# Taking weight remainders off GpSimd and laying out the order anew: attention, dense block and routed experts in one kernel

## The chip, the cores and the metric

The kernel runs on one core of a Trainium2 chip. The core has five engines with queues of their own: TensorE (PE in the profile, with PEld for its weight loads), VectorE (DVE), ScalarE (ACT), GpSimd (POOL) and SyncE (SP), which issues most of the transfers. The metric is the time of one execution on the device in microseconds, the median of several runs.

## The reference, cut to what matters

Three stages follow one another. Linear attention runs a state over 768 positions for 4 batches and 8 heads of 48. Its output, 3072 tokens of 384, goes through a dense block with a softplus between two matrices (384x2048 and 2048x384, given in double precision). Then every token is given to one of 8 experts with room for 384 tokens each, in the order of falling scores, and the expert's two matrices (384x1024 and 1024x384, with a relu) make the output.

```python
for t in range(S):                        # attention
    cur = np.einsum('bhd,bhe->bhde', u[None] * kt, vt)
    y[:, :, t] = np.einsum('bhd,bhde->bhe', rt, state + cur)
    state = w[None, :, :, None] * state + np.einsum('bhd,bhe->bhde', kt, vt)
...
h = x @ w_in                              # dense block
g = np.maximum(h, 0.0) + np.log1p(np.exp(-np.abs(h)))
x = g @ w_out
...
for idx in np.argsort(-logits.flatten()): # routing
    tok, e = (int(idx) // E, int(idx) % E)
    if assigned[tok] >= 0 or counts[e] >= cap:
        continue
    assigned[tok] = e
    counts[e] += 1
...
h = np.maximum(x[mask] @ w1[e], 0.0)      # one expert
out[mask] = h @ w2[e]
```

## The kernel before, in words

**Attention.** The 768 positions are cut into chunks of 64. One step handles a chunk for two batches, so there are 24 steps; step n belongs to token block n // 3 of the dense block (three steps, 384 tokens). A step loads r, k and v (`load_step`, on SyncE's queue), scales them with powers of the decay, turns them on TensorE, and forms the products of keys and queries inside the chunk: `prods`, line 524, 32 small matmuls. `masked` multiplies these products with a triangular mask on VectorE. For steps below `WHOLE` the products of both batches land in one half of the partitions and each of the two heads of a pair is masked by one instruction of 64x512 (line 532); for the later steps they are spread over both halves and masked by two instructions of 64x256 (line 537). Line 607 then makes the step's output, and lines 558 and 565 carry the state on.

**Dense block.** `ffn1` (lines 743 and 748) and `ffn2` (lines 855 and 858 to 860) run over 8 blocks of 384 tokens. Block 0 uses the weights in 32 bits, the later blocks use halves: a 16-bit value and a 16-bit remainder, three matmuls for one. The raw double-precision weights are loaded by SyncE and turned into 32 bits by three bit operations each on VectorE (lines 655, 657 and 659). The last twelve pieces of `ffn2` are kept for later (`LATE`): they fill TensorE while the routing starts.

**Routing and experts.** `select` runs eight rounds, one for each expert that is closed. A round is a chain of short VectorE instructions and small matmuls (lines 1108 and 1125) that finds the score at which the expert is full; then the chosen tokens are numbered and the numbering is inverted into a token list (VectorE lines 1205, 1196 and 1199, matmuls of line 1214, list at line 1223). The last round needs no search. `gather` fetches the listed rows with GpSimd (line 1277), SyncE transposes them (line 1352), `up` (line 1364) and `down` (lines 1382 to 1384) are the expert's matmuls, and `scatter` (line 1392) writes the rows out with GpSimd. `weights` loads an expert's matrices in eight tiles. ScalarE makes the 16-bit value of a tile (`hi`, line 1311), and VectorE the remainder (`lo`, line 1318). In rounds 6 and 7, for the seven tiles that `ON_POOL` names, it is otherwise: ScalarE scales the tile in place (line 1308) and casts it (line 1309), and GpSimd subtracts (line 1316).

**Order.** Every step is an `Item` with an engine (or a choice of ScalarE and VectorE), a planned duration, dependencies and a due time. `lay_out` is a list scheduler: it takes the engine that can start first and, of its items that can start within `SLACK`, the one that is due first. An item with a choice is delayed on an engine by `YIELD` and by `BIAS` times what the engine is slower. While a GpSimd item runs the plan doesn't start VectorE items on SBUF, unless the item is marked `remote`. The due times are made of the constants that stand in the code: `T0`, `LEN0`, `LEN` and `LAST` for the dense blocks, `STEP` and `SPAN` for the selection rounds and experts, and leads that end in L (`RAWL` for the raw loads of the dense weights, `BITL` for their bit operations, `HIL`, `LOL` and `FETCHL` for the experts' weights, `INVL` for the inversion). The order that comes out is written into the queues of the engines; on the chip each engine keeps it. Where the plan sees a gap on TensorE, `keep_warm` puts filler matmuls of 128x128 into it (line 143).

Of the kernel before, what the change touches and what calls it, by code (L numbers as in the profile page):

```python
# [14 lines left out]
OP = mybir.AluOpType  # L15
# [6 lines left out]
def tile_kernel(ctx, tc, r, k, v, w, u, w_in, w_out, w_gate, w1, w2, out):  # L22
# [18 lines left out]
    PE, ACT, DVE, POOL, SP = nc.tensor, nc.scalar, nc.vector, nc.gpsimd, nc.sync  # L41
# [11 lines left out]


    LAT = 150.0
    SLACK = 82.556
    SAME = {"dve": 130.0, "act": 150.0}
    NBANK = 7
    BIAS = 1.348
    YIELD0 = 247.951  # L60
    YIELD = {"dve": YIELD0}
    WARM = 1e9
    LPH = 6
# [45 lines left out]
    def op(eng, dur, fn, r=(), w=(), due=0.0, lat=None, bank=None, size=0.0, small=False):  # L109
        deps = []  # L110
        if lat is None:
            lat = LATA[0] if GROUP[0] == "att" else LAT
        for key in r:
            deps.append(writer.get(key))
        for key in w:
            deps.append(writer.get(key))
            deps += readers.get(key, [])
        for b in banks_of(bank):
            deps += b.items
        it = Item(eng, dur, fn, deps, due, lat, [b for b in banks_of(bank) if not b.items], bank, size)  # L120
        for b in banks_of(bank):
            if eng == "pe":
                b.items = [it]
            b.items = b.items[:1] if eng != "pe" else b.items
            b.all.append(it)
        it.small = small
        for key in r:
            readers.setdefault(key, []).append(it)
        for key in w:
            writer[key] = it  # L130
            readers[key] = []
        return it
# [115 lines left out]
        return 2 * pair, c * C  # L248


    T0 = 22576.265
    LEN0 = 52137.908
    LEN = 27173.331
    NLATE = 12
    EARLY = 0.549
    LATE = [divmod(NB * SPB - NLATE + i, SPB) for i in range(NLATE)]
    LAST = 21924.657


    SLOT = [0, 1, 2, 0, 1, 2, 0, 3]  # L260
# [1 line left out]
    def begins(blk):  # L262
        return T0 if blk <= 0 else T0 + LEN0 + (blk - 1) * LEN

# [6 lines left out]
            return ATT0 * t  # L271
        return begins(blk - 1) + lasts(blk - 1) * t / SPB - (AHEAD if blk > 1 else 0.0)

    AHEAD = 14956.929

    TURNED, TURN = 6, 1500.0
    WHOLE = 9
    SINGLE = 2
    COPIED = 6
    HALFL = 4425.245  # L280
    HALFL2 = 4963.628
    NLAT = 6
    LATL = 155.16
    OUTLATE = 12980.585
    RAWL = 12886.281
    BITL = 9483.311
    SPLITL = -3900.0
    WOUTL = 8511.548
    ATT0 = 2213.113
    LOADL = 1908.468  # L290

    base = begins(NB - 1) + LAST + 1000.0

# [47 lines left out]
    gate = work.tile([128, KC, 32], FT, name="gate")  # L341
# [24 lines left out]
    def load_step(n):  # L366
# [25 lines left out]
    wt = const.tile([128, HP], FT, name="wt")  # L392
    ut = const.tile([128, H * D], FT, name="ut")
    jp = keep.tile([128, 128], I32, name="jp")
    identf = keep.tile([128, 128], FT, name="identf")
    identh = keep.tile([128, 128], HF, name="identh")
    mask = const.tile([128, C], FT, name="mask")
# [10 lines left out]
                              for q in range(2)], w=["uq"], due=-1000.0, size=168.0)  # L408
    op("sp", 450.0, lambda: SP.dma_start(
        ut, bass.AP(tensor=u.tensor, offset=u.offset, ap=[[0, 128], [1, H * D]])), w=["ut"], due=due_att(3), size=1200.0)  # L410
    op("pool", 200.0, lambda: POOL.memset(gate, 0.0), w=["gate"], due=-1e9)
    op("sp", 450.0, lambda: SP.dma_start(gate[:, :, :E], w_gate.rearrange("(k p) e -> p k e", p=128)),
       w=["gate"], due=T0, size=168.0)
    op("pool", 100.0, lambda: POOL.iota(jp, pattern=[[1, 128]], base=0, channel_multiplier=-1), w=["jp"], due=-1e9)
# [1 line left out]
        for t in RS + KS:  # L416
            POOL.memset(t[:, :, D:], 0.0)

    op("pool", 700.0, pads, w=["pads"], due=-1e9)

    def masks():
        POOL.tensor_scalar(mask[0:64], jp[0:64, 0:64], 0.0, None, op0=OP.is_gt)
        POOL.tensor_scalar(mask[64:128], jp[64:128, 64:128], 0.0, None, op0=OP.is_gt)
        POOL.tensor_copy(identh, identf)

    op("pool", 800.0, lambda: POOL.tensor_scalar(identf, jp, 0.0, None, op0=OP.is_equal), r=["jp"], w=["ident"], due=-1e9)
    op("pool", 1500.0, masks, r=["jp", "ident"], w=["mask"], due=-1e9)


    def powers():  # L430
# [21 lines left out]
            DVE.tensor_mul(uw[q * 64:q * 64 + D, :, q], uq[q * 64:q * 64 + D], wt[q * 64:q * 64 + D])  # L452

    op("dve", 300.0, factors, r=["wt", "uq"], w=["uw"], due=2.5)
    op("dve", 1700.0, powers, r=["wt"], w=["pw", ("ar", 1, 0)], due=-1e8)

    def power_table(i):
        bank = Bank("att")
# [16 lines left out]
    def attention(n):  # L475
# [10 lines left out]
        if n % PC == 0:  # L486
            def zero():
                POOL.memset(X[x][0:64, 0], 0.0)
                POOL.memset(X[x][64:128, 1], 0.0)
            op("pool", 700.0, zero, w=[("st", x, 0), ("st", x, 1)], due=due)  # L490


        b1, b2 = Bank("att"), Bank("att")
# [34 lines left out]
        def masked(q):  # L528
            o = 1 - q
            if n < WHOLE:  # L530
                rows = slice(o * 64, (o + 1) * 64)
                DVE.tensor_mul(ar[rows, :, :, q, :], b3[q].view(HP, 2, 64)[rows],
                               mask[rows, None, None, :].to_broadcast([64, HP, 2, 64]))
                return
            for b in range(2):
                rows = slice(b * 64, (b + 1) * 64)
                DVE.tensor_mul(ar[o * 64:(o + 1) * 64, :, b, q, :], b3[q].view(HP, 64)[rows],
                               mask[rows, None, :].to_broadcast([64, HP, 64]))

        op("pe", 825.0 if n < WHOLE else 625.0, prods, r=[("kT", i), ("ar", i, 0), ("ar", i, 1)], w=[("am", i, 0), ("am", i, 1)], due=due + 3, bank=b3, small=True)  # L540
        for q in range(2):
            op("dve", 600.0 if n < WHOLE else 890.0, lambda q=q: masked(q), r=["mask"], w=[("am", i, q)], due=due + 3, bank=b3[q])


        if n % PC < PC - 1:
# [286 lines left out]

    NG = 1
    none = flat[0:64, 28:30].rearrange("p f t -> p (f t)")
    op("pool", 800.0, lambda: POOL.memset(none, 0.0), w=["none"], due=begins(0))
    for i in range(2 * NG):
        b0, s0 = step_tok(NS - NG + i // 2)
        X2S.append(op("sp", 650.0, lambda row=(b0 + i % 2) * S + s0: SP.dma_start(x2d[row:row + 64, :], none),
# [159 lines left out]
    def item(eng, dur, fn, deps, prio, lat=LAT, size=0.0, bank=None):  # L998
        take = [b for b in banks_of(bank) if not b.all]
        it = Item(eng, dur, fn, deps, prio, lat, take, bank, size)  # L1000
        for b in banks_of(bank):
            b.all.append(it)
        return it
# [4 lines left out]

    WQ, WB, RB = 4, 6, 4
    FIRST = 10500.0 + 8000.0 * NLATE  # L1010
    STEP = 21647.984
    SPAN = 23783.33

    ON_POOL = [()] * 6 + [(0, 1, 2, 3, 4, 5, 7)] * 2
    XLEAD = -13221.524
    GLEAD = 11385.847
    FETCHL = 13257.035
    W1L = -2788.168
    W2L = -1812.505
    HIL = 11584.279  # L1020
    LOL = 8711.69
    DOWNL = 7740.516
    INVL = -8223.999
    PUT = []
    IDX, EST, TK = {}, {}, {}
    SEL, WI, GI = {}, {}, {}
# [257 lines left out]
    def weights(p):  # L1284
        W[p] = [[None, None] for _ in range(2 * WQ)]
        z = {}

        def load():
            z["e"] = SP.value_load(EST[p][0:1, 0:1], min_val=0, max_val=E - 1)

        def fetch(y):
            e = z["e"]
            if y < WQ:
                q = F2 // WQ
                src = w1[bass.ds(e, 1)].rearrange("o (k p) f -> p (o k) f", p=128)[:, :, y * q:(y + 1) * q]
                sh = [128, KC, q]
            else:
                q = FB // WQ
                src = w2[bass.ds(e, 1)].rearrange("o (c p) m -> p (o c) m", p=128)[:, (y - WQ) * q:(y - WQ + 1) * q]
                sh = [128, q, DM]  # L1300
            z["raw", y] = moe.tile(sh, FT, name="mraw", bufs=RB)
            SP.dma_start(z["raw", y], src)
            z["sh", y] = sh

        def hi(y):
            W[p][y][0] = moe.tile(z["sh", y], HF, name="w1h" if y < WQ else "w2h", bufs=WB)
            if y in ON_POOL[p]:
                ACT.mul(z["raw", y], z["raw", y], 128.0)
                ACT.copy(W[p][y][0], z["raw", y])
            else:  # L1310
                ACT.mul(W[p][y][0], z["raw", y], 128.0)

        def lo(y):
            W[p][y][1] = moe.tile(z["sh", y], HF, name="w1l" if y < WQ else "w2l", bufs=WB)
            if y in ON_POOL[p]:
                POOL.tensor_tensor(W[p][y][1], z["raw", y], W[p][y][0], op=OP.subtract)
            else:
                DVE.scalar_tensor_tensor(W[p][y][1], z["raw", y], 128.0, W[p][y][0], op0=OP.mult, op1=OP.subtract)

        ld = item("sp", 700, load, [SEL[p][1], more_room], begin(p) - 15000)  # L1320
        WI[p] = []
        for y in range(2 * WQ):
            k = len(raws)
            old = raws[k - RB] if k >= RB else None
            want = begin(p) + (2930 * y - W1L if y < WQ else W2L + 2930 * (y - WQ))
            f = item("sp", 450, lambda y=y: fetch(y), [ld, old], want - FETCHL, size=1700)
            g = p * WQ + y % WQ - WB
            if g >= 0:
                gp, gz = divmod(g, WQ)
                wold = W1R[gp, gz] if y < WQ else W2R[gp, gz]  # L1330
            else:
                wold = []
            h = item("act", 1680 if y in ON_POOL[p] else 740, lambda y=y: hi(y), [f] + wold, want - HIL)
            if y in ON_POOL[p]:
                l = item("pool", 1660, lambda y=y: lo(y), [h] + wold, want - LOL)
            else:
                l = item("dve", 880, lambda y=y: lo(y), [h] + wold, want - LOL)
            raws.append(l)
            WI[p].append(l)

# [150 lines left out]
```

## Time and profile before

| | us |
|---|---|
| median of 3 runs | 761.86 |
| lowest and highest | 761.34, 764.19 |
| the profiled execution | 759.91 |
| its span, first to last instruction | 758.1 |
| TensorE busy in it | 741.5 |
| VectorE busy | 595.1 |
| ScalarE busy | 424.2 |
| GpSimd busy | 85.2 |

The profile is of one execution. Busy times of TensorE are of pipelined matmuls, so a matmul of 384 columns is shown with about 0.33 us though one starts every 0.16 us; a TensorE that is busy throughout is not for that reason at its peak. In the views below the time at the start of a row is counted from the span's start, the time behind it is the duration, and a bracket at the end names idle time of the engine just before and what ended it.

### The profile page before, as it was taken

The numbers are of one execution on the slowest core, as the hardware profiler recorded it, in microseconds if no ns is written. First come the engines' busy times: TensorE is split into PE (matmuls) and PEld (weight loads), VectorE is DVE, ScalarE is ACT, GpSimd is POOL, SyncE is SP. The second block draws the span as 40 slices with busy tenths as digits, with TensorE's granted clock in tenths as the row PEclk, the third lists the DMA queues.
The fourth block names the chain that finished last, engine by engine and source line by source line (L and its number), as shares of the span: only waits on it lengthen the run. The fifth ranks groups of instructions, "written<-read, shape, count | busy, mean of one in ns | idle before, by whom it ended". The sixth has DMA issues, their size and how long they took to land.

```text
span 758.1 us, 18115 instructions
## 1 busy us (share of the span) xinstructions
PE 741.5 (98%) x7144; PEld 489.2 (65%) x7144; DVE 595.1 (79%) x1594; ACT 424.2 (56%) x859; POOL 85.2 (11%) x114
## 2 busy tenths in 40 slices
PE   9999999999999999999999999999999999997996
PEld 8767766666666666667666666666666666664663
DVE  6899999998777777778988768787798889984220
ACT  4586766776766666668989702120343533462741
POOL 2000000000000000000001000000532122145641
PEclk9999999999999999999999999999999999998998
DMA  5896884243333333331110005142487382855810
GB/s 107 194 214 164 163 204 114 48 84 74 64 64 63 64 64 64 63 64 34 32 23 2 1 22 151 59 146 74 102 196 204 107 231 92 219 159 134 208 53 32
DMA packets 164853, 78.86 MB, mean 104 GB/s; under 512 B 130464, under 2 KB 160416, under 8 KB 164768
## 3 DMA queue, kind: packets, MB, share of 16 engines
q1 hardware_dynamic: 161696, 68.26, 38.9%
q0 software_dynamic: 3072, 9.44, 3.9%
q8 instruction: 56, 0.92, 0.5%
q14 instruction: 29, 0.24, 0.1%
HBM read 60.37 MB, written 9.63 MB: 92 GB/s over the span
## 4 chain that ended last, share of the span: by engine, by line
PE 71%; DVE 15%; issue 5%; DMA 3%; POOL 2%; ACT 2%; SPq 1%; POOLq 0%; DVEq 0%; ACTq 0%
PE bank L748 19%; PE bank L1364 9%; PE bank L858 6%; PE bank L860 6%; PE bank L859 6%; PE bank L1382 3%; PE bank L1383 3%; PE bank L1384 3%; PE bank L607 2%; PE bank L1108 2%; PE bank L855 2%; PE bank L524 1%; DMA third<-moe_w_in 1%; PE bank L558 1%; SPq L373 1%
## 5 line engine op out<-in xcount | busy, mean ns | idle before, releaser
L748 PEld LDWEIGHTS <-wi 128*128 128x128 f16 x1008 | 97.9, 98 | 66.0 <-issue 2.3
L748 PE MATMUL bank<-xt,wi 128*128 128x384 f16 x672 | 127.6, 326 | 0.1
L754 ACT ACTIVATE ta<-bank 128x384 f32<-128x384 f32 x128 | 61.4, 483 | 36.3 <-PE bank L748 25.1
L761 DVE SCALAR_TENSOR_TENSOR gf<-bank,ta 128x384 f32<-128x384 f32 x112 | 61.4, 550 | 21.9 <-ACT ta L756 21.6
L858 PE MATMUL bank<-wo,g 128*128 128x384 f16 (+1 forms) x240 | 78.5, 327 | 0.0
L860 PE MATMUL bank<-wo,g 128*128 128x384 f16 (+1 forms) x240 | 78.5, 327 | 0.0
L859 PE MATMUL bank<-wo,g 128*128 128x384 f16 (+1 forms) x240 | 78.4, 327 | 0.0
L748 PE MATMUL bank<-xs,wi 128*128 128x384 f16 x336 | 72.9, 326 | 0.0
L1364 PE MATMUL bank<-g,w1h 128*128 128x384 f16 x384 | 72.9, 326 | 0.0
L755 ACT ACTIVATE ta<-ta 128x384 f32<-128x384 f32 x128 | 66.4, 522 | 2.5
L756 ACT ACTIVATE ta<-ta 128x384 f32<-128x384 f32 x128 | 66.2, 521 | 2.2
L1382 PE MATMUL bank<-w2h,g 128*128 128x384 f16 x192 | 63.7, 332 | 0.0
L1383 PE MATMUL bank<-w2l,g 128*128 128x384 f16 x192 | 63.7, 332 | 0.0
L1384 PE MATMUL bank<-w2h,g 128*128 128x384 f16 x192 | 63.6, 331 | 0.0
L1368 ACT ACTIVATE g<-bank 128x384 f16<-128x384 f32 x64 | 31.2, 489 | 41.2 <-PE bank L1364 24.7
L768 DVE SCALAR_TENSOR_TENSOR g<-gf,g 128x384 f16<-128x384 f32 x80 | 43.9, 552 | 11.3 <-ACT g L351 10.8
L1364 PEld LDWEIGHTS <-w1h 128*128 128x128 f16 x384 | 35.7, 98 | 22.1
L351 ACT ACTIVATE x2o<-bank 128x384 f16<-128x384 f32 x24 | 11.6, 489 | 67.5 <-PE bank L860 41.5
L1371 DVE SCALAR_TENSOR_TENSOR g<-bank,g 128x384 f16<-128x384 f32 x64 | 34.0, 548 | 18.9 <-ACT g L1368 18.8
L1277 POOL DMA_INDIRECT third<-x2d,idx x24 | 27.6, 1151 | 156.7 <-PE bank L1125 132.3
L351 ACT ACTIVATE g<-gf 128x384 f16<-128x384 f32 x66 | 34.3, 520 | 16.2 <-DVE gf L761 16.0
L1364 PE MATMUL bank<-g,w1l 128*128 128x384 f16 x192 | 41.7, 326 | 0.0
(237 smaller groups left out, 1511.6 us busy)
## 6 DMA issues: line engine op xcount, KB each, us to landing
mraw<-moe_w SPq DMA_DIRECT2D x64, 384.0 KB, 3.9
third<-moe_w_in SPq DMA_DIRECT2D x16, 384.0 KB, 4.7
third<-moe_w_out SPq DMA_DIRECT2D x8, 768.0 KB, 4.8
kn<-k SPq DMA_DIRECT2D x48, 96.0 KB, 3.0
rn<-r SPq DMA_DIRECT2D x48, 96.0 KB, 3.4
vn<-v SPq DMA_DIRECT2D x48, 96.0 KB, 3.0
x2d<-x2o SPq DMA_DIRECT2D x48, 96.0 KB, 2.2
X<-v SPq DMA_DIRECT2D x36, 96.0 KB, 3.4
```

Source lines behind the costliest of these rows:

```text
L748: PE.matmul(ph, WF[:, f, a, kk, :], x[:, kk, :], start=(i == 0), stop=(i == 3 * KC - 1))
L754: op("act", 371.0, lambda: ACT.activation(ta, bank.view(BT), AF.Abs), w=[("ta", c)], due=due, bank=bank)
L755: op("act", 413.0, lambda: ACT.activation(ta, ta, AF.Exp, scale=-1.0), w=[("ta", c)], due=due)
L756: op("act", 413.0, lambda: ACT.activation(ta, ta, AF.Ln, bias=1.0), w=[("ta", c)], due=due)
L761: op("dve", 470.0, lambda: DVE.scalar_tensor_tensor(gf, bank.view(BT), 0.0, ta, op0=OP.max, op1=OP.add), r=[("ta", c)], w=[("gf", c)], due ...
L858: PE.matmul(p, gh[:, f, ts], WU[:, f, 0, :no], start=(f == 0), stop=False)
L859: PE.matmul(p, gh[:, f, ts], WU[:, f, 1, :no], start=False, stop=False)
L860: PE.matmul(p, gl[:, f, ts], WU[:, f, 0, :no], start=False, stop=(f == FC - 1))
L1364: PE.matmul(ph, a[:, kk, fs], XH[p][:, x0 + kk, :], start=(i == 0), stop=(i == 3 * KC - 1))
L1382: PE.matmul(po, h1h[:, f, js], w2h[:, fz, :], start=(f == 0), stop=False)
L1383: PE.matmul(po, h1h[:, f, js], w2l[:, fz, :], start=False, stop=False)
L1384: PE.matmul(po, h1l[:, f, js], w2h[:, fz, :], start=False, stop=(f == FB - 1))
```

## The change

The change takes the remainders of rounds 6 and 7 from GpSimd: `ON_POOL` is gone, and all tiles are made as in rounds 0 to 5, one ScalarE instruction and one VectorE instruction. `WHOLE` goes from 9 to 3, so that steps 3 to 8 use the products and masks of the later steps. The planned durations of seven kinds of item are new, four memset items are marked `remote`, and 29 constants of the ordering have new values. The computation is otherwise the same, instruction by instruction, but for what the planner chooses anew: order, engine of the items with a choice, and filler.

```diff
-    SLACK = 82.556
+    SLACK = 106.939
-    BIAS = 1.348
-    YIELD0 = 247.951
+    BIAS = 2.396
+    YIELD0 = 49.069
...
-    T0 = 22576.265
-    LEN0 = 52137.908
-    LEN = 27173.331
+    T0 = 22458.956
+    LEN0 = 56876.682
+    LEN = 30310.245
...
-    WHOLE = 9
+    WHOLE = 3
...
-    RAWL = 12886.281
-    BITL = 9483.311
+    RAWL = 17811.751
+    BITL = 3671.703
...
-    LOADL = 1908.468
+    LOADL = -407.377
...
-    op("pool", 200.0, lambda: POOL.memset(gate, 0.0), w=["gate"], due=-1e9)
+    op("pool", 200.0, lambda: POOL.memset(gate, 0.0), w=["gate"], due=-1e9).remote = True
...
-    op("pool", 700.0, pads, w=["pads"], due=-1e9)
+    op("pool", 700.0, pads, w=["pads"], due=-1e9).remote = True
...
-    op("pool", 800.0, lambda: POOL.tensor_scalar(identf, jp, 0.0, None, op0=OP.is_equal), r=["jp"], w=["ident"], due=-1e9)
-    op("pool", 1500.0, masks, r=["jp", "ident"], w=["mask"], due=-1e9)
+    op("pool", 560.0, lambda: POOL.tensor_scalar(identf, jp, 0.0, None, op0=OP.is_equal), r=["jp"], w=["ident"], due=-1e9)
+    op("pool", 1350.0, masks, r=["jp", "ident"], w=["mask"], due=-1e9)
...
-    op("dve", 1700.0, powers, r=["wt"], w=["pw", ("ar", 1, 0)], due=-1e8)
+    op("dve", 2300.0, powers, r=["wt"], w=["pw", ("ar", 1, 0)], due=-1e8)
...
-            op("pool", 700.0, zero, w=[("st", x, 0), ("st", x, 1)], due=due)
+            op("pool", 850.0, zero, w=[("st", x, 0), ("st", x, 1)], due=due).remote = True
...
-        op("pe", 825.0 if n < WHOLE else 625.0, prods, r=[("kT", i), ("ar", i, 0), ("ar", i, 1)], w=[("am", i, 0), ("am", i, 1)], due=due + 3, bank=b3, small=True)
+        op("pe", 1078.0 if n < WHOLE else 625.0, prods, r=[("kT", i), ("ar", i, 0), ("ar", i, 1)], w=[("am", i, 0), ("am", i, 1)], due=due + 3, bank=b3, small=True)
...
-            op("dve", 600.0 if n < WHOLE else 890.0, lambda q=q: masked(q), r=["mask"], w=[("am", i, q)], due=due + 3, bank=b3[q])
+            op("dve", 714.0 if n < WHOLE else 890.0, lambda q=q: masked(q), r=["mask"], w=[("am", i, q)], due=due + 3, bank=b3[q])
...
-    STEP = 21647.984
-    SPAN = 23783.33
-
-    ON_POOL = [()] * 6 + [(0, 1, 2, 3, 4, 5, 7)] * 2
+    STEP = 27547.175
+    SPAN = 9996.08
...
-    INVL = -8223.999
+    INVL = -22194.544
...
-            if y in ON_POOL[p]:
-                ACT.mul(z["raw", y], z["raw", y], 128.0)
-                ACT.copy(W[p][y][0], z["raw", y])
-            else:
-                ACT.mul(W[p][y][0], z["raw", y], 128.0)
+            ACT.mul(W[p][y][0], z["raw", y], 128.0)
...
-            if y in ON_POOL[p]:
-                POOL.tensor_tensor(W[p][y][1], z["raw", y], W[p][y][0], op=OP.subtract)
-            else:
-                DVE.scalar_tensor_tensor(W[p][y][1], z["raw", y], 128.0, W[p][y][0], op0=OP.mult, op1=OP.subtract)
+            DVE.scalar_tensor_tensor(W[p][y][1], z["raw", y], 128.0, W[p][y][0], op0=OP.mult, op1=OP.subtract)
...
-            h = item("act", 1680 if y in ON_POOL[p] else 740, lambda y=y: hi(y), [f] + wold, want - HIL)
-            if y in ON_POOL[p]:
-                l = item("pool", 1660, lambda y=y: lo(y), [h] + wold, want - LOL)
-            else:
-                l = item("dve", 880, lambda y=y: lo(y), [h] + wold, want - LOL)
+            h = item("act", 740, lambda y=y: hi(y), [f] + wold, want - HIL)
+            l = item("dve", 870, lambda y=y: lo(y), [h] + wold, want - LOL)
```

## Rows read from the trace of the kernel before

**Rows 1.** Busy time by stage: window, its length, PE, PEld, DVE, ACT, POOL, PEclk, DMA.

```profile
0.00:32.00 32.00, 29.56 (x523) 27.30 (x523) 24.30 (x66) 14.58 (x30) 4.25 (x17) 1.00 0.67 141
32.00:130.00 98.00, 96.65 (x1081) 66.92 (x1078) 94.56 (x184) 70.87 (x157) 0.00 (x0) 1.00 0.77 176
541.00:683.50 142.50, 142.50 (x1038) 89.64 (x1035) 124.79 (x406) 64.52 (x108) 41.87 (x50) 1.00 0.62 170
683.50:689.60 6.10, 0.57 (x5) 0.26 (x4) 6.07 (x5) 2.65 (x5) 5.30 (x5) 0.94 0.85 181
689.60:695.70 6.10, 6.10 (x30) 3.24 (x30) 2.05 (x7) 0.00 (x0) 0.00 (x0) 0.50 0.62 170
695.70:751.50 55.80, 55.80 (x344) 33.43 (x342) 11.38 (x19) 25.10 (x41) 26.32 (x28) 1.00 0.37 100
```

**Rows 2.** The same view for the filler of line 143 alone (PE, PEld, PEclk, DMA).

```profile
0.00:32.00 32.00, 13.93 (x170) 12.66 (x170) 1.00 0.67 141
```

**Rows 3.** Timeline of TensorE: the first matmuls after the hole.

```profile
689.59 0.85 PE L1214 MATMUL bank<-rv,cmi 128*128 128x24 bf16 x12 [5.53 <-DVE rv L1199]
```

**Rows 4.** Timeline of VectorE around 683 us.

```profile
682.11 0.96 DVE L1205 TENSOR_TENSOR cmi<-slot,sqd 128x1536 bf16<-128x1536 bf16 x1
...
683.45 5.51 DVE L1196 TENSOR_TENSOR aj<-jj,sqd 128x144 bf16<-128x144 f32 x1
```

**Rows 5.** Two lines over the whole span: durations in ns, lowest, median, highest.

```profile
L1196 DVE TENSOR_TENSOR aj<-jj,sqd x8: 291/300/5514, 465.0 to 683.4; 128x144 bf16<-128x144 f32 x8
...
L1199 DVE TENSOR_TENSOR rv<-aj,val x16: 311/322/1767, 465.3 to 689.2; 128x144 bf16<-128x144 bf16 x16
```

**Rows 6.** Timeline of GpSimd around 683 us.

```profile
681.73 0.96 POOL L1277 DMA_INDIRECT third<-x2d,idx  x1 [0.30 <-issue]
...
683.97 1.65 POOL L1316 TENSOR_TENSOR w1l<-mraw,w1h 128x768 f16<-128x768 f32 x1
685.57 3.22 POOL L1316 TENSOR_TENSOR w2l<-mraw,w2h 128x768 f16<-128x768 f32 x2
```

**Rows 7.** Groups of instructions by line: count, busy us, mean ns, idle before.

```profile
L1316 POOL TENSOR_TENSOR w1l<-mraw,w1h 128x768 f16<-128x768 f32 x8 | 13.1, 1650 | 4.3 <-ACT w1h L1309 4.2
...
L1308 ACT ACTIVATE mraw<-mraw 128x768 f32<-128x768 f32 x14 | 11.7, 834 | 0.0
...
L1318 DVE SCALAR_TENSOR_TENSOR w1l<-mraw,w1h 128x768 f16<-128x768 f32 x24 | 22.8, 949 | 0.6 <-ACT w1h L1311 0.4
```

**Rows 8.** The two forms of the mask over the span, durations as in rows 5.

```profile
L532 DVE TENSOR_TENSOR ar<-bank,mask x18: 675/688/695, 14.1 to 112.0; 64x512 f32<-64x512 f32 x18
...
L537 DVE TENSOR_TENSOR ar<-bank,mask x60: 405/422/429, 131.1 to 384.4; 64x256 f32<-64x256 f32 x60
```

**Rows 9.** Timeline of TensorE: the products of a step in either form.

```profile
108.84 1.15 PE L524 MATMUL bank<-ar,kT 64*64 64x64 f32 x32
...
211.65 0.69 PE L524 MATMUL bank<-ar,kT 64*64 64x64 f32 x32
```

**Rows 10.** Timeline of SyncE's queue in the lead-in: raw weight loads.

```profile
15.26 3.71 SPq L665 DMA_DIRECT2D third<-moe_w_in  x4
```

**Rows 11.** Timelines of VectorE and GpSimd at 3.90 us.

```profile
3.90 0.16 DVE L437 TENSOR_TENSOR sq<-sq 128x4 f32<-128x4 f32 x1
...
3.90 0.41 POOL L489 MEMSET X<- 64x384 f32 x1
```

**Rows 12.** Timelines: starts of two selection rounds, round 6's last transpose, its experts' first matmuls.

```profile
632.82 0.33 DVE L1048 TENSOR_REDUCE c<-LG 128x24 f32<-128x192 f32 x1
...
670.83 0.34 DVE L1048 TENSOR_REDUCE c<-LG 128x24 f32<-128x192 f32 x1
...
687.40 1.23 SPq L1352 DMA_TRANSPOSE g<-third  x1
...
704.61 1.14 PE L1364 MATMUL bank<-g,w1h 128*128 128x384 f16 x6
```

**Rows 13.** Issues of transfers: operation, count, median us to landing.

```profile
g<-third SPq DMA_TRANSPOSE x21, 3.9
```

More of the change, by code (lines that the diff above doesn't have):

```diff
@@ L248, in step_tok @@
         return 2 * pair, c * C
-    T0 = 22576.265
-    LEN0 = 52137.908
-    LEN = 27173.331
+    T0 = 22458.956
+    LEN0 = 56876.682
+    LEN = 30310.245
     NLATE = 12
-    EARLY = 0.549
+    EARLY = 0.718
     LATE = [divmod(NB * SPB - NLATE + i, SPB) for i in range(NLATE)]
-    LAST = 21924.657
+    LAST = 18038.602
     SLOT = [0, 1, 2, 0, 1, 2, 0, 3]
@@ L272, in due_att @@
         return begins(blk - 1) + lasts(blk - 1) * t / SPB - (AHEAD if blk > 1 else 0.0)
-    AHEAD = 14956.929
+    AHEAD = 10423.766
     TURNED, TURN = 6, 1500.0
-    WHOLE = 9
+    WHOLE = 3
     SINGLE = 2
     COPIED = 6
-    HALFL = 4425.245
-    HALFL2 = 4963.628
+    HALFL = 6043.115
+    HALFL2 = -2605.37
     NLAT = 6
-    LATL = 155.16
-    OUTLATE = 12980.585
-    RAWL = 12886.281
-    BITL = 9483.311
+    LATL = 121.181
+    OUTLATE = 12383.246
+    RAWL = 17811.751
+    BITL = 3671.703
     SPLITL = -3900.0
-    WOUTL = 8511.548
-    ATT0 = 2213.113
-    LOADL = 1908.468
+    WOUTL = 8403.536
+    ATT0 = 2153.936
+    LOADL = -407.377
     base = begins(NB - 1) + LAST + 1000.0
@@ L834, in tile_kernel @@
     none = flat[0:64, 28:30].rearrange("p f t -> p (f t)")
-    op("pool", 800.0, lambda: POOL.memset(none, 0.0), w=["none"], due=begins(0))
+    op("pool", 800.0, lambda: POOL.memset(none, 0.0), w=["none"], due=begins(0)).remote = True
     for i in range(2 * NG):
@@ L1010, in tile_kernel @@
     FIRST = 10500.0 + 8000.0 * NLATE
-    STEP = 21647.984
-    SPAN = 23783.33
-    ON_POOL = [()] * 6 + [(0, 1, 2, 3, 4, 5, 7)] * 2
[L1015 to L1022, printed above, removed]
-    INVL = -8223.999
+    STEP = 27547.175
+    SPAN = 9996.08
+    XLEAD = -13198.5
+    GLEAD = 9878.544
+    FETCHL = 15087.31
+    W1L = -2479.166
+    W2L = 3350.21
+    HIL = 11522.076
+    LOL = 7006.972
+    DOWNL = 8214.33
+    INVL = -22194.544
     PUT = []
```

## The prediction

> **What bounds the kernel now.** I read the busy time by stage first [rows 1]. TensorE is busy in all of 32 to 130 us (96.65 of 98) and again from 689.6 us to 751.5 us. Busy alone could hide slow matmuls, so I read three things beside it: how much of it is filler, the granted clock of each stretch, and the waits. Filler (the 128x128 bf16 matmuls on "still" that the plan puts into gaps which it foresees, line 143) is 13.93 us in the first 32 us [rows 2]: there TensorE waits for loads and for VectorE. After that it is a string of matmuls without holes, with one exception. At 683.5 us it stops, and the next instruction starts at 689.59 us after 5.53 us of idle time that ended on VectorE, line 1199 [rows 3]. The granted clock is 0.50 from 689.6 to 695.7 us (the lower of the two levels, 1.2 GHz), after 6.1 us in which TensorE did 0.57 us of work, and 1.00 again afterwards [rows 1]. So the kernel is bound by TensorE, and what can be won lies in three places: the first 32 us, the hole at 683 us with the slow stretch behind it, and TensorE work that becomes shorter.
>
> **Where the hole comes from.** On VectorE the instruction of line 1196 starts at 683.45 us and takes 5.51 us [rows 4]; the same instruction has a median of 300 ns over its eight calls [rows 5]. The GpSimd engine runs three elementwise weight remainders of line 1316 in 683.97 to 688.79 us [rows 6], and VectorE gets on when the third ends. Its instruction has two inputs in SBUF, and so has line 1199, whose longest call took 1767 ns against a median of 322 [rows 5]. A GpSimd gather doesn't do this: line 1205, also with two inputs, took 0.96 us [rows 4] while a gather ran from 681.73 us [rows 6]. TensorE has its matmuls in a fixed order, and the twelve of line 1214 stand ahead of the down projection, which was ready; so all of TensorE waits.
>
> **Part 1, no remainders on GpSimd in rounds 6 and 7.** Fourteen GpSimd instructions of 1.65 us go, one for each of the fourteen tiles that ScalarE scales in two passes [rows 7]. Without them line 1196 takes 0.30 us and the two of line 1199 0.32 us each, so line 1214 could start at about 683.45 + 0.30 + 0.64 + 0.1 = 684.5 us in place of 689.59. Gain: 5.1 us. About 0.4 us of wait stays, and the clock should not fall for that. The slow stretch behind goes too: from the first down matmul at about 690.3 to 695.7 us TensorE ran at half speed, which costs half of 5.4 us, 2.7 us. Together 7.8 us, on the path that sets the end, because TensorE has no further hole up to 751.5 us [rows 1].
> What it adds: fourteen remainders on VectorE at 0.95 us (as line 1318 has them [rows 7]), 13.3 us. About half, seven of round 6, fall in 671 to 706 us, the others later. VectorE was held there for some 7.5 us by GpSimd, which comes back, and from 695.7 to 751.5 us it is busy 11.38 of 55.8 us [rows 1]. So it is hidden by idle time of VectorE; if it is not, the price is rival 1. ScalarE loses one pass of 0.83 us for each of them [rows 7], 11.7 us, and the path of a tile from raw to ready shrinks from 0.83 + 0.83 + 1.65 to 0.83 + 0.95 us. I cost that at nothing: no matmul waited for a weight there. SyncE's weight loads are freed by the remainder that ends earlier; they can only move forward.
>
> **Part 2, large masks only in the first three steps.** Steps 3 to 8 change form. VectorE: two instructions of 688 ns become four of 422 [rows 8], 1.69 in place of 1.38 us, so 0.31 us more a step, 1.9 us for six. TensorE: the 32 products of a step take 1.15 us in the old form and 0.69 in the new [rows 9], 0.46 us less, 2.7 us for six. All six lie in 32 to 130 us, where TensorE is busy 96.65 of 98 us, but VectorE is busy 94.56 of them too [rows 1]. Bounds: a gain of 2.7 us if TensorE alone decides, a loss of 1.9 us if VectorE does. TensorE is nearer to being full, yet VectorE has only 3.4 us left; I take a gain of 1.3 us.
>
> **Part 3, the ordering.** All due times move (STEP, SPAN, LEN, the leads), the two choices between ScalarE and VectorE are weighted anew (BIAS up, YIELD0 down), seven planned durations change (the mask to 714, the products to 1078, the powers to 2300 ns), and memsets no longer block VectorE in the plan. It adds no instruction; it moves nearly all. The trace of before can't show a new order, so I bound it by stage. Lead-in: weight loads get a due time some 5 us earlier against the attention loads on SyncE's queue, where four of them take 3.71 us [rows 10], while their bit operations on VectorE get one some 6 us later. That is 3.7 us lost or as much won; of the 13.93 us of filler no more than 7.7 us could be won, the idle time of VectorE [rows 1]. The two edits work against each other, so I take 0. From 32 to 683 us nothing can be won, and a new order can only open holes: from 0 up to the size of the one known, 7.8 us. I take 0, since the order of before, laid out by the same planner, has but one, and it came from VectorE being held by GpSimd longer than anything else there was late.
>
> One rule of the Trainium skill speaks against the new mark on the memsets. What the row shows: a VectorE multiply with two SBUF inputs took 0.16 us at 3.90 us while a GpSimd memset ran from 3.90 to 4.31 us [rows 11]. The Trainium skill, "GPSIMD Engine Reference", section 8 (Key points), says that GpSimd shares its SBUF interfaces with VectorE and contends with VectorE instructions that have two SBUF inputs; it makes no exception for memsets. By that rule VectorE would stand still for each of some four such memsets of 0.41 us, and the sum would be 1.6 us higher, 754.4 us; by the row the mark is right and costs nothing. For elementwise work the trace agrees with the rule, for memsets and gathers it doesn't. I give the rule 2 in 100, inside the forecast's own range.
>
> **Sum.** The profiled execution took 759.91 us (span 758.1). 759.9 - 7.8 - 1.3 + 0 = 750.8 us. The median of the runs lies 1.95 us above the profiled one, so I forecast 752.8 us; own range 748.5 to 757.
>
> **Rivals.**
> 1. The hole stays, smaller. If the plan puts three of the moved remainders ahead of round 7's inversion (lines 1205, 1196, 1199), as three stood ahead on GpSimd, TensorE waits 2.9 us there, with or without the 2.7 us of slow clock. Time: 752.8 + 2.9 = 755.7 to 758.4 us, about 757. For it: VectorE is busy 6.07 of 6.1 us in that stretch. Against it: the inversion's due time is moved forward by the new INVL.
> 2. VectorE becomes the bound in 32 to 130 us. It has 3.4 us left; the masks take 1.9. Each evacuation moved to it from ScalarE costs 0.55 to 0.69 us, so from the third one on it is late, and ten would make TensorE wait about 4.5 us. With no gain from part 2: 759.9 - 7.8 + 4.5 + 1.95 = 758.6 us. For it: YIELD0 falls from 248 to 49. Against it: BIAS rises, and a full VectorE hands work to ScalarE, which has a quarter of that stage free.
> 3. Slower: the selection runs out of lead. The experts need a round's token list. The last full round began at 632.82 us and its successor at 670.83: 38.0 us a round [rows 12]. The experts did five and a half rounds in 541 to 683.5 us (the up projection of the sixth had just ended), 25.9 us a round [rows 1]. The lead therefore shrinks by some 12 us a round. The last transpose of round 6's tokens was issued in 687.40 to 688.63 us [rows 12]; such an issue lands a median of 3.9 us after its start [rows 13], so the tokens are there at 691.3; without the hole its experts start 7.8 us before 704.61 [rows 12], at 696.8. The margin is 5.5 us. If each of the four rounds from 559 us on gets d longer under the new due times, TensorE loses 4d - 5.5 us and 2.7 us of clock. It decides from d = 1.4 us, and the result is slower by over 0.5% from d = 3.9. At d = 5: 752.8 + 20 - 5.5 + 2.7 = 770 us. For it: a round is some forty VectorE instructions that each wait for whatever runs there, and the due times of both sides change. Against it: the moved remainders lie behind round 6's list.
> 4. More than forecast. If the lead-in wins its 3.7 us and the masks their 2.7: 752.8 - 3.7 - 1.4 = 747.7, or less, about 747 us.
> That the change doesn't do what it says can be left aside for part 1, for no GpSimd remainder can be left; for the due times it is rivals 2 and 3.
>
> **How the numbers follow.** Forecast 0.46, rival 1 0.17, rival 2 0.12, rival 3 0.14, rival 4 0.11. About 0.5% (3.8 us) is what a measurement here can tell from no change: faster is under 758.05 us, slower above 765.7. Faster: 0.46 + 0.11 + 0.10 of rival 1 + 0.03 of rival 2 = 0.70. Same: the rest of rivals 1 and 2, 0.16. Slower: 0.14. The range of 745 to 763 us takes in the forecast, rivals 1, 2 and most of 4, and leaves rival 3 out.
>
> **What would show it.** Right: in 660 to 700 us no idle time of TensorE over 1 us, granted clock 1.00 throughout, line 1196 never above 0.4 us, no instruction of the GpSimd remainder; steps 3 to 8 with products of 0.69 us; no new wait between 32 and 683 us; the first block's first matmul (line 743) within 4 us of 32 us. Wrong: a stretch with a clock of 0.50 elsewhere, an expert round that waits for its transposes, or idle time of TensorE on VectorE between 32 and 130 us.

## The result and the profile after

| | before | after |
|---|---|---|
| time, median (7 runs each, same call) | 763.81 us (761.34 to 764.91) | 756.13 us (753.80 to 758.76) |
| ratio, with 95% interval | | 0.9905 (0.9883 to 0.9926) |
| the profiled execution: time, span | 759.91, 758.1 us | 756.81, 755.0 us |

The kernel became faster by 0.7 to 1.2%. The medians differ by 7.7 us, but the two profiled executions by only 3.1. Why the gap is so wide is the subject of one experiment below.

The busy time by stage of the kernel after (window, its length, PE, PEld, DVE, ACT, POOL, PEclk, DMA); the stretch of the old hole is cut out finely:

```profile
32.00:130.00 98.00, 97.19 (x1041) 65.37 (x1040) 95.15 (x191) 70.16 (x151) 0.00 (x0) 1.00 0.71 172
...
541.00:683.50 142.50, 140.12 (x1014) 87.83 (x1012) 118.95 (x395) 58.23 (x99) 36.06 (x45) 0.99 0.60 163
...
671.00:683.50 12.50, 12.50 (x86) 7.68 (x85) 10.07 (x45) 6.09 (x10) 2.09 (x3) 1.00 0.49 158
683.50:690.00 6.50, 6.50 (x43) 3.88 (x41) 5.95 (x18) 3.42 (x6) 2.91 (x3) 1.00 0.55 133
690.00:696.00 6.00, 6.00 (x46) 3.92 (x45) 5.07 (x10) 1.22 (x2) 2.68 (x4) 1.00 0.88 178
696.00:704.60 8.60, 8.60 (x55) 5.18 (x53) 2.76 (x5) 3.89 (x6) 4.11 (x7) 1.00 1.12 283
```

TensorE is busy in all of 671 to 704.6 us at a granted clock of 1.00; where it did 0.57 us of work in 6.10, and then ran at 0.50 [rows 1], it now does 6.50 in 6.50. But 541 to 683.5 us, full before, has lost 2.4 us. The line that had been held [rows 4, 5], over the whole span (lowest, median, highest ns; lines of the kernel after lie up to 11 lower, so 1196 is 1195 and 1214 is 1213), and then TensorE's waits (total, times, longest us):

```profile
L1195 DVE TENSOR_TENSOR aj<-jj,sqd x8: 298/302/302, 463.7 to 689.1; 128x144 bf16<-128x144 f32 x8
```

```profile
PE bank L1107 <- DVE cmp L1094: 2.2, 1, 2.2
PE bank L1396 <- DMA third<-x2d,idx: 1.2, 1, 1.2
```

The longest of its eight calls went from 5514 to 302 ns, and line 1213 is no longer among the waits. The longest wait is now another, 2.2 us at line 1107 (1108 before), a matmul of the search in a selection round. The first profile of before did not have it. Around it, by stretch:

```profile
549.00:552.00 3.00, 2.92 (x20) 1.66 (x18) 0.80 (x4) 0.48 (x2) 1.25 (x3) 1.00 1.08 242
552.00:555.00 3.00, 0.84 (x10) 0.39 (x9) 2.72 (x6) 2.61 (x6) 0.00 (x0) 1.00 1.09 167
555.00:556.00 1.00, 1.00 (x9) 0.57 (x8) 1.00 (x3) 0.00 (x0) 0.00 (x0) 0.81 0.91 289
556.00:560.00 4.00, 4.00 (x18) 2.03 (x17) 2.91 (x12) 1.22 (x2) 0.00 (x0) 0.62 0.67 178
```

TensorE does 0.84 us of work in 552 to 555 us, and from 555 to 560 us the granted clock is 0.81 and 0.62, where it was 1.00 throughout before. What starts it is on ScalarE: the engine sits idle for 4.18 us before a relu (line 1357), whose matmuls of line 1353 had ended at 547.9 us. VectorE is late there too (it starts line 1115 at 548.43 us, 2.0 us after its matmuls ended). GpSimd's gather of 1.71 us at 546.26 us is no sign of it: the same gather took 1.70 us in the first profile of before, where nothing was late.

```profile
546.84 0.49 ACT L1357 ACTIVATE g<-bank 128x384 f16<-128x384 f32 x1 [0.88 <-PE bank L1107]
551.52 0.49 ACT L1357 ACTIVATE g<-bank 128x384 f16<-128x384 f32 x1 [4.18 <-PE bank L1353]
```

### The profile page after: what moved, and what is told of

Same layout as the page of the kernel before. It is cut to its first block, busy times and chain, and to the rows that moved or that the text cites. A ratio compares the mean times of both kernels' runs of the same rounds, so it can differ in the third digit from the quotient of the medians.

```text
span 755.0 us, 18145 instructions
## 1 busy us (share of the span) xinstructions
PE 740.8 (98%) x7153; PEld 487.3 (65%) x7153; DVE 621.4 (82%) x1693; ACT 388.5 (51%) x772; POOL 62.0 (8%) x100
## 4 chain that ended last, share of the span: by engine, by line
PE 69%; issue 12%; DVE 9%; POOL 3%; ACT 3%; DMA 2%; SPq 1%; POOLq 0%; DVEq 0%; ACTq 0%
PE bank L748 20%; PE bank L858 7%; PE bank L860 7%; PE bank L859 7%; PE bank L1353 6%; PE bank L855 3%; PE bank L607 2%; PE bank L1371 2%; PE bank L1372 2%; PE bank L1373 2%; PE bank L1107 2%; PE bank L743 2%; PE bank L524 2%; POOL out L1381 1%; POOL third L1276 1%
## 5 line engine op out<-in xcount | busy, mean ns | idle before, releaser
L1310 DVE SCALAR_TENSOR_TENSOR w2l<-mraw,w2h 128x768 f16<-128x768 f32 x32 | 30.4, 953 | 10.5 <-ACT w2h L1306 8.3
```

## The experiments

The theory: the gain is the hold that GpSimd's subtractions put on VectorE's two-input instructions, and that alone. The rivals: the new order closes the hole, or the masks bring a share.

**The hold by itself.** The order of before is kept to the instruction; each GpSimd subtraction is cut to its first 16 columns, and a memset writes the rest.

```diff
-POOL.tensor_tensor(W[p][y][1], z["raw", y], W[p][y][0], op=OP.subtract)
+POOL.tensor_tensor(W[p][y][1][:, :, :16], z["raw", y][:, :, :16], W[p][y][0][:, :, :16], op=OP.subtract)
+POOL.memset(W[p][y][1][:, :, 16:], 0.0)
```

> The kernel before with its order kept: every GpSimd remainder of rounds 6 and 7 subtracts only the first 16 of its columns and fills the rest with zeros by a memset, so most of the remainder is left out. Hold theory (VectorE instructions with two SBUF inputs are held by the subtraction, and the hole of TensorE at 683 us is that hold): line 1196 falls to about 0.3 us, the hole falls under 1 us, the clock stays at 1.00, and the time falls by 7 to 8 us (ratio about 0.990). Order theory (the gain of the change comes from the new order and the hole would be filled by something else that is late there): TensorE still waits at least 3 us at line 1214 and the time falls by less than 3 us.

Measured: 0.9900 (0.9885 to 0.9914), 756.36 us. All of the gain is there, with the old plan, the old masks and the scaling still done twice on ScalarE. Line 1196 over the span, and VectorE and GpSimd where a cut subtraction and its memset meet the two calls of line 1199, in this kernel:

```profile
L1196 DVE TENSOR_TENSOR aj<-jj,sqd x8: 293/301/346, 466.2 to 688.7; 128x144 bf16<-128x144 f32 x8
...
681.42 0.62 DVE L1199 TENSOR_TENSOR rv<-aj,val 128x144 bf16<-128x144 bf16 x2
...
681.55 0.31 POOL L1316 TENSOR_TENSOR w1l<-mraw,w1h 128x48 f16<-128x48 f32 x1 [2.15 <-ACT w1h L1309]
681.81 0.69 POOL L1317 MEMSET w1l<- 128x720 f16 x1
```

The hold is gone (346 ns at most). The two calls of line 1199 take 0.62 us together, with the cut subtraction (681.55 to 681.86 us) and the first 0.23 us of a memset beside them; an undisturbed pair takes 0.54 us (the row at 689.60 us in the next experiment). What makes the 0.08 us more can't be told from the rows. The Trainium skill, "SBUF — State Buffer", section "Who interferes with whom", says that a VectorE instruction with two SBUF inputs contends with a GpSimd instruction that reads SBUF and not with one that only writes it. For memsets [rows 11] agree, with a multiply of 0.16 us inside a memset of 0.41 us; the rows here overlap too little to add to that.

**More of it.** The reverse: every subtraction is issued twice.

```diff
 POOL.tensor_tensor(W[p][y][1], z["raw", y], W[p][y][0], op=OP.subtract)
+POOL.tensor_tensor(W[p][y][1], z["raw", y], W[p][y][0], op=OP.subtract)
```

> The kernel before with its order kept: every GpSimd remainder of rounds 6 and 7 is subtracted twice. Hold theory: the three subtractions beside line 1196 become six, so its time goes from 5.5 to about 10.4 us, the hole of TensorE from 5.5 to about 10.4 us, and the time rises by 5 us or somewhat more (ratio 1.006 to 1.012). Order theory: the hole stays at 5.5 us, and the time moves by less than 2 us, unless weights come late.

Measured: 1.0011 (0.9996 to 1.0025), 764.53 us. The expectation was missed, and the reason is instructive. VectorE and GpSimd from 679 to 691 us, the same line 1156 in the kernel before (over its whole span), and TensorE's waits:

```profile
679.64 2.00 DVE L1199 TENSOR_TENSOR rv<-aj,val 128x144 bf16<-128x144 bf16 x2
683.20 1.63 DVE L1156 TENSOR_TENSOR closed<-closed,esel 128x8 f32<-128x8 f32 x1
...
689.27 0.30 DVE L1196 TENSOR_TENSOR aj<-jj,sqd 128x144 bf16<-128x144 f32 x1
689.60 0.54 DVE L1199 TENSOR_TENSOR rv<-aj,val 128x144 bf16<-128x144 bf16 x2
...
679.77 1.68 POOL L1316 TENSOR_TENSOR w1l<-mraw,w1h 128x768 f16<-128x768 f32 x1 [2.15 <-ACT w1h L1309]
681.53 1.66 POOL L1317 TENSOR_TENSOR w1l<-mraw,w1h 128x768 f16<-128x768 f32 x1
683.14 1.67 POOL L1316 TENSOR_TENSOR w1l<-mraw,w1h 128x768 f16<-128x768 f32 x1
...
690.02 0.95 POOL L1277 DMA_INDIRECT third<-x2d,idx  x1 [0.30 <-issue]
690.99 1.65 POOL L1316 TENSOR_TENSOR w1l<-mraw,w1h 128x768 f16<-128x768 f32 x1
```

```profile
L1156 DVE TENSOR_TENSOR closed<-closed,esel x8: 166/167/1128, 458.7 to 678.3; 128x8 f32<-128x8 f32 x8
```

```profile
PE bank L1384 <- POOL w2l L1317: 4.9, 1, 4.9
...
PE bank L1214 <- DVE rv L1199: 1.2, 1, 1.2
```

In the round before the last, lines 1199 (2.00 us for two) and 1156 (1.63 us) are held, as they were in the kernel before (1767 ns [rows 5] and 1128 ns at most). In the last round line 1196, held there before, escapes with 0.30 us: GpSimd makes its gathers behind four subtractions in a row, the last gather starts at 690.02 us, and the next subtraction at 690.99, when the inversion on VectorE is through. The hole at line 1214 shrank to 1.2 us, while TensorE waited 4.9 us elsewhere, for a remainder that GpSimd made too late. So the hold is real, but which instruction it hits is a coincidence of two queues; the price is not proportional to the work.

**The three parts.** Each part alone, and two of the three pairs: part 1 is `ON_POOL = [()] * 8` in the old plan, part 2 is `WHOLE = 3` in it; part 3 is the changed kernel with both taken back; parts 1 and 3, the changed kernel with `WHOLE = 9`.

> The kernel before with part 1 alone: all remainders on VectorE, every constant, mask and duration as before. Hold theory: no hole at line 1214 over 1 us, time lower by 7 to 8 us (ratio about 0.990), that is the whole gain of the change. Rival (remainders on VectorE stand ahead of the inversion): a hole of 2 to 3 us is left and the gain is 3 to 5 us. Order theory: gain under 2 us.

> The kernel before with part 2 alone: large masks in the first three steps only, everything else as before. If TensorE decides in 32 to 130 us: products of steps 3 to 8 at 0.69 us in place of 1.15, time lower by 2.7 us (ratio 0.9965). If VectorE decides there: no gain, up to 1.9 us lost (ratio 1.000 to 1.0025), and the time saved on the products comes back as filler or waits between 32 and 130 us. The hole at line 1214 stays in both cases unless the shift of a few us takes the VectorE instruction away from the GpSimd subtractions.

> The changed kernel with the remainders back on GpSimd and the large masks back in the first nine steps, so that only the ordering (due times, durations, remote marks) differs from before. Hold theory: no gain of its own, the time is within 3 us of before, with a hole beside the GpSimd subtractions wherever a VectorE instruction with two SBUF inputs meets them. Order theory: the time falls by 5 us or more.

> The changed kernel with the large masks back in the first nine steps (parts 1 and 3 without 2). If the masks gain 1 to 3 us, this is slower than the changed kernel by as much (ratio to before 0.992 to 0.994). If VectorE takes the gain back, it equals the changed kernel (ratio 0.990 to 0.991).

> The kernel before, its ordering numbers and durations untouched, with no GpSimd remainders and large masks only in the first three steps. The remainder theory: as part 1 alone, 0.991 of the kernel before (756 to 758 us), no hole at the first state matmul after the fifth expert, and nothing visible for the masks. Rival, the ordering carries part of the gain: 0.994 or above. Rival, the masks gain once the remainder is out of the way: 0.989 or below.

| kernel | ratio to before (95%) | median, us | wait at line 1214, us | wait at line 1108, longest, us |
|---|---|---|---|---|
| part 1 alone | 0.9913 (0.9896 to 0.9929) | 756.90 | none | 2.0 |
| part 2 alone | 1.0011 (0.9995 to 1.0026) | 763.30 | 5.5 | 0.6 |
| part 3 alone | 0.9970 (0.9957 to 0.9983) | 760.99 | 2.8 | 2.3 |
| parts 1 and 3 | 0.9924 (0.9903 to 0.9945) | 756.56 | none | 2.0 |
| parts 1 and 2 | 0.9918 (0.9896 to 0.9941) | 756.98 | none | 2.3 |
| all three | 0.9905 (0.9883 to 0.9926) | 756.13 | none | 2.2 |

Part 1 gives the gain, and nothing that is added to it can be told from nothing. Part 3 alone gains 0.3%: the new order moves the subtractions a little against the inversion. VectorE and GpSimd in that kernel:

```profile
688.33 0.30 DVE L1196 TENSOR_TENSOR aj<-jj,sqd 128x144 bf16<-128x144 f32 x1
688.66 4.24 DVE L1199 TENSOR_TENSOR rv<-aj,val 128x144 bf16<-128x144 bf16 x2
...
689.25 3.24 POOL L1316 TENSOR_TENSOR w1l<-mraw,w1h 128x768 f16<-128x768 f32 x2
```

Line 1196 is through, line 1199 is held by two subtractions in place of three (until 692.9 us, they end at 692.49), and 2.8 us of the hole are left, without a slow stretch behind it (clock 1.00 in 690 to 696 us). This profile has a slow stretch elsewhere, 0.76 in 57 to 64 us, which parts 1 and 3 and the changed kernel don't have (1.00), so the 0.3% is not the price of the hole alone. With part 1 there is no hole left to shrink. So much for the rival that the order closes the hole: it halves it.

Why the masks bring no gain there is seen in part 2 alone, 32 to 130 us (first row the stage, second the filler in it; PE, PEld, then PEclk and DMA):

```profile
32.00:130.00 98.00, 96.11 (x1080) 65.75 (x1081) 94.19 (x186) 67.19 (x147) 0.00 (x0) 1.00 0.74 172
...
32.00:130.00 98.00, 7.13 (x63) 4.70 (x63) 1.00 0.74 172
```

TensorE is as busy as in [rows 1], but 7.13 us of it is filler; a row like [rows 2] for this stage of the kernel before reads

```profile
32.00:130.00 98.00, 3.71 (x23) 1.93 (x20) 1.00 0.77 176
```

The matmul time that the small masks save, some 2.7 us, came back as 3.4 us of filler, which the plan puts where it foresees TensorE waiting. A busy TensorE that holds filler is not a full TensorE. How far the work has come is seen in the last start of line 748, the end of the dense block's first matrix (durations in ns, then first and last start; kernel before, part 2 alone, parts 1 and 3, all three):

```profile
L748 PE MATMUL bank<-xs,wi x336: 326/326/327, 89.2 to 428.6; 128*128 128x384 f16 x168
...
L748 PE MATMUL bank<-xs,wi x336: 326/326/327, 87.8 to 430.5; 128*128 128x384 f16 x168
...
L748 PE MATMUL bank<-xs,wi x336: 326/326/326, 86.0 to 430.7; 128*128 128x384 f16 x168
...
L748 PE MATMUL bank<-xs,wi x336: 326/326/326, 82.9 to 429.2; 128*128 128x384 f16 x168
```

In the old order the small masks make this end 1.9 us later, which is the bound of the prediction for the case that VectorE decides; in the new order they make it 1.5 us earlier. Second profiles of the kernel before and of the changed kernel both have 428.6 us, so single profiles differ here by up to 0.6. What the masks are worth seems to hang on the order, but in the times neither shift is clear of noise: parts 1 and 3 came out at 0.9924, where they were expected if the masks gain, and their interval holds the 0.9905 of all three as well.

**Why the profiles differ by less than the medians.** The kernel before, unchanged, profiled a second time.

> The kernel before, unchanged, for a second profile. The other profiles taken so far all have a wait of TensorE of 2 to 3 us near 552 us, behind a relu of ScalarE (the fourth of the first expert) that starts 3.6 us after its matmuls ended; the first profile of before has none. If that wait is a matter of the single execution, this profile has it too, has the hole of about 5.5 us at line 1214 as well, and a span of about 762 us. If it belongs to the edits, this profile has no such wait and a span of about 758 us.

One run of 763.64 us, next to a median of 763.00 in that call. Its waits, and 552 to 560 us by stretch:

```profile
PE bank L1214 <- DVE rv L1199: 5.5, 1, 5.5
PE bank L1108 <- DVE cmp L1095: 2.0, 1, 2.0
```

```profile
552.00:555.00 3.00, 0.98 (x11) 0.58 (x10) 2.75 (x7) 2.17 (x5) 0.00 (x0) 1.00 0.77 165
555.00:560.00 5.00, 5.00 (x23) 2.54 (x22) 3.84 (x15) 1.22 (x2) 0.00 (x0) 0.66 0.70 182
```

The wait at line 1108 is not made by the change: the kernel before has it too, with the slow stretch. The execution that the prediction was read from happened to be without it. Two matmuls of either profile, first the one that waits and then one behind it (first profile, then second):

```profile
551.70 0.41 PE L1108 MATMUL bank<-oh,cmp 128*128 128x32 bf16 x6
554.24 0.33 PE L1384 MATMUL bank<-w2h,g 128*128 128x384 f16 x1
...
554.29 0.45 PE L1108 MATMUL bank<-oh,cmp 128*128 128x32 bf16 x6 [2.02 <-DVE cmp L1095]
...
558.49 0.38 PE L1384 MATMUL bank<-w2h,g 128*128 128x384 f16 x1
```

The second profile is 2.6 us behind at the wait and 4.3 us after the slow stretch; up to 548 us the two run level to 0.3 us, and at the end they are 3.7 us apart. So the wait with its slow stretch is the difference of the two spans, and the half clock makes 1.7 us of it. Like against like, 763.64 to 756.81 is a gain of 6.8 us.

**What makes that wait.** Two kernels ask whether the gathers of the second round, whose rows come in beside the transposes of the first expert, make the relu late. The first lets them wait for the last of the eight blocks of that expert's up projection, the second for the fourth (VectorE's half of it; "fourth quarter" below means this block). A third was to leave out the filler of the late part, to see what that costs.

```diff
+later = W1R[0, WQ - 1] if p == 1 else []
-GI[p].append(item("pool", 1270, ..., [SEL[p][3], old, more_room] + need, ...
+GI[p].append(item("pool", 1270, ..., [SEL[p][3], old, more_room] + need + later, ...
```

In the second kernel `later` is `phs[3:4] if p == 1 else []`. The third, as it ran, is the changed kernel itself, to the instruction: the edit isn't in it, and it has the same 18 filler matmuls behind 500 us (536.0 to 540.7 us). So nothing was measured of what the filler costs. It serves as a second run and a second profile of the changed kernel.

> The changed kernel with the gathers of the second expert round held back until the last up projection of the first round, so that they no longer run beside the first round's gathers, transposes and weight loads. If the crowd of transfers at 545 to 552 us makes the late relu: the wait near 552 us and the slow clock behind it go, and the time falls by 3 to 4 us against the changed kernel (ratio to before about 0.986). If the late relu has another cause: the wait stays and the time is within 1 us of the changed kernel (ratio about 0.990).

> The changed kernel with the gathers of the second round put behind the fourth quarter's matmuls of the first expert, so that only a single round's gathers run beside that expert's transposes. If these transfers cause the late relu at 549 to 555 us: its lateness falls from 3.6 us to under 2 us, no half clock behind it, and the time is 2 to 4 us less (0.986 to 0.988 of the kernel before), unless the gathers then come late for the second round. If the lateness has another cause: relu still over 3 us late and 0.990 to 0.992.

> The changed kernel without the few filler matmuls that the plan puts behind 500 us (TensorE idles there instead). If the filler is only cover for waits: the same time as the changed kernel, 0.990 to 0.992 of the kernel before, with TensorE idle under 1 us more in the late part. If the filler costs time of its own: up to 0.5 us less. If the clock needs it: a stretch at half clock in the late part and 2 us or more longer.

The first: 0.9996 (0.9982 to 1.0010), 762.33 us. The wait fell to 0.6 us and the clock stayed at 1.00, but the plan now foresees late tokens and fills the gaps; the filler in 541 to 683.5 us went from 0.52 us to

```profile
541.00:683.50 142.50, 10.35 (x158) 9.22 (x158) 1.00 0.60 155
```

which is more than the wait had cost; that the filler takes the gain back is argued from this row, no run shows it apart. The second adds a single filler matmul to the plan: 0.9875 (0.9856 to 0.9893), 753.62 us (753.17 to 754.29), the lowest median of the study. The changed kernel in the same call (the third): 0.9903 (0.9874 to 0.9933), 755.15 us (753.57 to 760.92), with its 2.2 us wait. The two intervals overlap, so that the second beats the changed kernel, by some 0.2%, is likely, not settled. The second's relu, its longest wait on VectorE's compare and 549 to 560 us:

```profile
549.12 0.49 ACT L1358 ACTIVATE g<-bank 128x384 f16<-128x384 f32 x1 [2.52 <-PE bank L1124]
```

```profile
PE bank L1107 <- DVE cmp L1094: 0.6, 1, 0.6
```

```profile
549.00:552.00 3.00, 2.72 (x17) 1.42 (x15) 2.13 (x6) 2.58 (x5) 0.87 (x2) 1.00 0.64 187
552.00:555.00 3.00, 2.66 (x21) 1.76 (x22) 2.86 (x10) 1.33 (x4) 0.00 (x0) 1.00 0.73 198
555.00:560.00 5.00, 4.97 (x32) 2.70 (x31) 4.63 (x20) 1.01 (x2) 0.57 (x1) 1.00 0.93 202
```

The relu's idle time fell from 4.18 (4.06 in the second profile of the changed kernel) to 2.52 us, the wait to 0.6, and the clock stays at 1.00 here, as expected if the gathers are the cause. But one profile can't credit that to the move: part 2 alone, which doesn't have it, shows 2.51 us and a wait of 0.6 as well. Of the eleven profiles without the move nine have a wait of 2.0 to 2.6 us there; of the three with it, none. The last experiment makes the same move in the kernel before.

> The kernel before, its remainders, masks and ordering numbers untouched, with the gathers of the second round put behind the fourth quarter's matmuls of the first expert. If the late relu of the first expert comes from these transfers and is a cost of its own, apart from the remainders: no half clock at 550 to 560 us, 2 to 4 us less than the kernel before (0.995 to 0.997), and the 5 us hole at the first state matmul after the fifth expert stays. If the gain of the same move in the changed kernel came from elsewhere: 0.998 to 1.002.

Measured: 1.0013 (0.9989 to 1.0038), 760.75 us, no gain. It does not decide the matter: this call ran on another chip, where the kernel before took a median of 759.42 us instead of 763 to 764, so it may have had no such wait to lose; that kernel was not profiled there. The profile of the moved kernel has the full hole (5.5 us at line 1214) and no wait at line 1108. What makes ScalarE and VectorE late at 547 us in most profiles stays open. That the share of busy DMA engines is high there does not suffice: the first profile of before had 1.17 and 1.26 in 552 to 560 us with no engine late, against 1.09 in the changed kernel.

## Why the prediction was right

The forecast was 752.8 us in a range of 745 to 763, its own range 748.5 to 757; measured was 756.13, faster, as the chance of 0.70 had it. By the steps of the prediction:

- **Where the hole comes from, and part 1** (7.8 us): right. Removing the hold alone gives 0.9900, part 1 alone 0.9913, 7.4 and 6.8 us on medians; 7.8 lies inside both intervals. One thing the rows leave open: line 1196 starts 0.52 us ahead of the first subtraction [rows 4, 6], more than the 0.30 us that it takes unheld, so when the hold sets in can't be read from them. The signs for this part came: no idle time of TensorE in 671 to 704.6 us, a clock of 1.00, line 1195 at 302 ns at most.
- **What part 1 adds** (nothing): right. VectorE took over the fourteen remainders, and no matmul waits for a weight in the late part.
- **Part 2** (1.3 us): the size was wrong; alone the masks gave 1.0011 (0.9995 to 1.0026), no gain. The choice between the two bounds went by which engine was busier, but 3.71 us of TensorE's busy time there were filler, which the prediction's own first step says is to be read apart; for this stage it was not. In the old order the profile shows the other bound, 1.9 us lost up to 428 us.
- **Part 3** (0): right in sum, with part 1 in place (0.9905 for all three, 0.9918 without part 3). The first matmul of line 743 starts at 31.16 us, 0.95 us before the 32.11 of the kernel before; the filler in 32 to 130 us rose from 3.71 to 5.11 us, and a new wait of 1.2 us on a gather (line 1396) came. The bound "from 0 up" for this part left out that the order alone could take away half of the hole (part 3 alone, 0.9970).
- **From profile to median** (1.95 us): wrong size, and the larger of the two errors. It was 3.9 us (759.91 to 763.81), because the profiled execution lacked the wait at line 1108, which makes 3.7 us between the two profiles. With 0 for the masks and 3.9 here the sum is 759.9 - 7.8 + 3.9 = 756.0 us; that it meets 756.13 so closely is partly luck, for the terms are known to about 1 us.
- **"No new wait between 32 and 683 us"**: it failed, and a sign of being wrong came, a half clock elsewhere (0.62 in 556 to 560 us). The wait at line 1107 and that stretch are of the kernel before too; the 1.2 us at line 1396 are new.
- **Rivals.** Rival 1 (a smaller hole) did not come: no wait at line 1213. Rival 2 came in part: part 2 gained nothing, as it says, but the 4.5 us of waiting did not come. TensorE is busy for 97.19 of 98 us in 32 to 130 us, and of that 5.11 are filler, 1.4 more than before; the last matmul of line 748 starts at 429.2 us against 428.6. Rival 3: the last two rounds that begin with the large reduction are 38.28 us apart, 0.27 more than before [rows 12] and far from the 1.4 from which it decides; round 6's experts start earlier than in [rows 12], at 701.42 us:

```profile
639.85 0.34 DVE L1047 TENSOR_REDUCE c<-LG 128x24 f32<-128x192 f32 x1
678.13 0.34 DVE L1047 TENSOR_REDUCE c<-LG 128x24 f32<-128x192 f32 x1
...
701.42 1.14 PE L1353 MATMUL bank<-g,w1h 128*128 128x384 f16 x6
```

- **The rule weighed against the memsets**: no memset held VectorE visibly, as the row had it; the prediction gave the rule 1.6 us, which is too little to be told from noise in the time.

## What to carry to other kernels

Look at the longest call of an instruction beside its median: 5514 against 300 ns pointed straight to the gain, and it was worth the stall plus the half-clock stretch behind it. Read filler apart in every stage before calling an engine the bound, or time saved on it comes back as filler. And profile the kernel before twice: a wait that only some executions have shifts the step from profile to median by more than the small terms of the sum.

## What the runs showed of the hardware

- A held VectorE instruction is not let go between two GpSimd instructions: line 1196 waited through three subtractions in a row [rows 4, 6]. With the subtractions placed otherwise (part 3 alone, doubled subtractions) line 1196 took 0.30 us; in part 3 alone line 1199 was held in its place, 4.24 us for two calls.
- Idle time of about 2 us on TensorE does not always cost clock, not even in one and the same kernel: after the wait of 2.2 us the granted clock was 0.62 to 0.81 in the first profile of the changed kernel, and 1.00 in its second, after a wait of the same length. The spans are 755.0 and 752.8 us. Of the nine profiles with that wait four show the fall. The second:

```profile
552.00:555.00 3.00, 1.06 (x11) 0.79 (x12) 2.93 (x7) 1.82 (x4) 0.00 (x0) 1.00 0.80 150
555.00:560.00 5.00, 4.97 (x32) 2.78 (x30) 4.71 (x19) 1.22 (x2) 0.00 (x0) 1.00 0.80 204
```

- The same kernel took a median of 759.42 us in one call and of 763.0 to 763.8 us in the others, on other chips, 0.5% apart, as much as some of the effects in question; only ratios within one call are safe.
